# Sixteen first-product units and four block products as 64-row halves on both halves of the array

## The chip, the cores and the metric

The kernel runs on one core of one Trainium2 chip. That core has five engines with instruction queues of their own: PE (TensorE, the 128x128 matmul array, with a separate weight load that the profile lists as PEld), DVE (VectorE), ACT (ScalarE), POOL (GpSimd) and SP (SyncE, which here only starts DMAs). Matmuls write to PSUM, which has eight banks; DVE and ACT read results from there.

The metric is the device time of one execution in microseconds (us), as the median of several runs. A profile is one further execution under the hardware profiler. Its page and its trace give the span from the first to the last instruction.

## The reference

Attention over normalised queries and keys, and behind it a dense block with a hard-swish between its two products. In outline:

```python
# q, k, v: (batch 8, heads 12, seq 448, head_dim 64); tau = 0.1
q_n = q / (norm(q) + 1e-6)
k_n = k / (norm(k) + 1e-6)
scores = q_n @ k_n.T / tau
attn = softmax(scores)                 # with 1e-9 beside the sum
o = attn @ v
x = o as rows of tokens                # (3584, 768): 8 batches of 448 tokens
# w_in: (768, 2048), w_out: (2048, 768)
h = x @ w_in                           # "first product"
g = h * clip(h + 3, 0, 6) / 6
out = g @ w_out                        # "second product"
```

## The kernel before

**Units.** The work behind the attention is cut into units, and each unit is a run of matmuls into one PSUM bank, followed by what empties the bank.

- A *first-product unit* (`mm1_unit`, matmuls at L598) makes one of the 16 blocks of 128 columns of `h` for one batch: six matmuls (768 = 6 x 128 rows) of 128 rows by 448 tokens into one bank. ACT then computes `u = relu(h/6 + 0.5)` from the bank (`relu`, L614), and DVE computes `min(u, 1) * h` from `u` and the bank (`product`, L620) into `g`. Only after that is the bank free.
- The second product is done by a scheme with seven block products for a pair of token blocks, where eight would be usual. Sums and differences of blocks of `g` (`g_sum`, DVE, L772) and of `w_out` come first. A *block product* (`product_unit`, matmuls at L794) is eight matmuls of 128 rows by 384 columns. Its name has a digit 1 to 7 and the number of the pair: 2.9 is block product 2 of pair 9. Products 2, 5 and 6 accumulate in the bank that holds 4, 3 and 1 of the same pair. Product 1 is added to a buffer by DVE (L851), 6 and 7 are added by DVE into an output tile that is stored (L819), 2 to 5 are copied by ACT (L813, L842), and POOL combines buffers (L823 to L827).
- A *single unit* (`single_unit`, L874) is 16 matmuls for half the columns of one token block that has no partner.

**Banks.** Two of the eight banks hold the attention's values (PV). The other six (M0, M1, Y, Z, M2, M3 in this order) form a ring: each new unit that does not accumulate takes the next bank (`next_bank`, L160, through `bank_of`, L321). A matmul into a bank that is still being read waits for the reader.

**Order.** Each engine executes its queue in the order in which the program issues it; nothing is scheduled later. The order of the attention's start is a written list (`PLAN`), then a loop goes over pairs of heads and mixes units into the attention by `TURNS`. Behind the last attention stands the list `units[NP]` (L984 to L993), which is run by `whole_units` (L1034): it issues a unit's matmuls and then at once the instructions that empty its bank (`post`, one list each for ACT, DVE and POOL). Dependencies between engines become semaphore waits where the data require them.

The part of `units[NP]` that the change touches (L987 to L989) runs, in this order: first-product unit 0 of the last batch, block product 2.9, unit 1, 1.9, unit 2, 7.9, unit 3, 6.9, and then units 4 to 15 one behind the other. The two single units `s6.0` and `s6.1` follow, with DVE's sums for pair 10 between them, and then the block products of pairs 10 and 11, which read what the 16 first-product units made.

**Halves in the kernel before.** A matmul may use 64 of the array's 128 rows. The attention's scores (L445) do: the contraction is 64 long, and two matmuls of 64 rows, one on rows 0 to 63 and one on rows 64 to 127, stand beside one another in the queue, into two banks. Part of the values (L486) do the same.

Of the kernel before, what the change touches and what calls it, by code (L numbers as in the profile page):

```python
# [64 lines left out]
def kernel(  # L65
# [10 lines left out]
    nc = tc.nc  # L76
    B, H, S, D = q.shape
# [4 lines left out]
    NP = B * HP  # L82
    CC = d_model // 128
    FCN = d_ff // 128
# [17 lines left out]
    w_in_sb = const.tile([128, CC, d_ff], BF16, name="w_in_sb", tag="w_in_sb")  # L102
# [4 lines left out]
    KC = FCN // 2  # L107
# [60 lines left out]
    def needs(*what):  # L168
        for w in what:
            assert w in issued or any(x < 0 for x in w[1:] if isinstance(x, int)), w  # L170

    halves = {}
# [148 lines left out]
    def bank_of(name, reads):  # L321

        bank = {"Y": Y, "Z": Z}[name] if name else next_bank()
        key = id(bank)
        assert not unread.get(key), name
        unread[key] = reads
        return bank, key
# [228 lines left out]

    evac_n = [0]
    post = {"a": [], "v": [], "p": []}
    g_done = set()

    def tail(c, n):
# [8 lines left out]
    def g_of(b):  # L570
        if b == B - 1:
            needs(("NM", NP - 1), ("RE", NP - 1), ("VC", NP - 1))
            return g_last
        return gT[b % 2]
# [16 lines left out]
    def mm1_unit(b, fc, ends=None):  # L591
        needs(*(("CX", i) for i in range(b * HP, (b + 1) * HP)))
        assert len(weights) <= 8 - 2 * min(2, 4 * fc // FCN)
        x, g, c0 = xT[b % 2], g_of(b), b % 2 * SR
        ps, key = bank_of(None, 1)
        def products_of(ccs):
            for cc in ccs:
                nc.tensor.matmul(  # L598
                    ps[:, 0:S],
                    w_in_sb[:, cc, fc * 128 : (fc + 1) * 128],  # L600
                    x[:, cc, 0:S],
                    start=(cc == 0),
                    stop=(cc == CC - 1),
                )

        if ends is None:
            products_of(range(CC))
        else:
            products_of(range(CC - 1))
            ends.append(lambda: products_of([CC - 1]))  # L610

        def relu():
            u = sb.tile([128, S], BF16, name="u", tag="u", bufs=3)
            nc.scalar.activation(  # L614
                out=u[:, :], in_=ps[:, 0:S], func=AF.Relu, bias=0.5, scale=1.0 / 6.0
            )
            post["v"].append(lambda: product(u))

        def product(u):
            nc.vector.scalar_tensor_tensor(  # L620
                out=g[:, fc, c0 : c0 + S],
                in0=u[:, :],
                scalar=1.0,
                in1=ps[:, 0:S],
                op0=ALU.min,
                op1=ALU.mult,
            )
            unread[key] = 0
            g_done.add((b, fc))

        post["a"].append(relu)
# [78 lines left out]
    def sum_of(n, what):  # L710

        if what == "e":
            return late_sums[1]["e"]
        if n < LOOP or n == LAST:
            return gs[what + str(n % 2 if n not in (3, 5) else 0) if what == "7" else what]
        return late_sums[n % 2][what]
# [32 lines left out]
    def block(n, i, k):  # L749
        if PAIRS[n][i] == (2, 2):  # L750
            return kept[k]
        return half(*PAIRS[n][i], k)
# [22 lines left out]
    def product_unit(n, name, end=None, apart=False):  # L775

        need = {"3": ["y3"], "4": ["y4"], "1": "1", "6": "6", "7": "7"}.get(name, [])
        assert all((x, c) in summed for x in need for c in range(KC))
        if name not in "34":
            assert (n, name) in g_summed  # L780
        base = None if apart else {"2": "4", "5": "3", "6": "1"}.get(name)
        if base is None:
            banks[n, name] = bank_of(None, 1)
        ps, key = banks.pop((n, base)) if base else banks[n, name]
        c0, width = (MH // 2 * end, MH // 2) if end in (0, 1) else (0, MH)
        if name in "167":
            lhs, rhs = sum_of(n, name), w_sum[name]
        else:
            i, k = {"3": (0, 0), "4": (1, 1), "2": (1, 0), "5": (0, 1)}[name]
            m = LEFT if name in "42" else RIGHT  # L790
            lhs, rhs = block(n, i, k), w_out_sb[:, :, m].rearrange("p (c k) m -> p c k m", k=2)[:, :, k, :]
        m = ps[:, c0 : c0 + width]
        for c in range(KC):
            nc.tensor.matmul(  # L794
                m,
                lhs[:, c, :],
                rhs[:, c, c0 : c0 + width],
                start=(base is None and c == 0),
                stop=(c == KC - 1),
                skip_group_check=True,  # L800
            )
        issued_products.add((n, name))
        d, e = d_and_e(n)
        if base is None and name in "34":
            unread[key] = 1 + ((n, name) not in APART)

        def done(i, o, cols):
            unread[key] = 0
            result(*PAIRS[n][i], cols, o, end)

        def copied(i, cols):
            o = out_tile()
            nc.scalar.copy(out=o[:, :], in_=m)  # L813
            parts[n, name] = o
            done(i, o, cols)

        def added(i, cols, x):
            parts[n, name] = o = out_tile()
            nc.vector.tensor_tensor(out=o[:, 0:width], in0=m, in1=x[:, c0 : c0 + width], op=ALU.add)  # L819
            done(i, o, slice(cols.start + c0, cols.start + c0 + width))  # L820

        def both():
            nc.gpsimd.tensor_tensor(out=e, in0=d, in1=e, op=ALU.add)  # L823
            nc.gpsimd.tensor_tensor(out=d, in0=e, in1=parts[n, "5"][:, :], op=ALU.subtract)

        def rest():
            nc.gpsimd.tensor_tensor(out=e, in0=e, in1=parts[n, "2"][:, :], op=ALU.subtract)  # L827

        def added_later(i, cols, x):
            parts[n, name] = o = out_tile()  # L830
            nc.scalar.copy(out=o[:, :], in_=m)
            unread[key] = 0

            def add():
                nc.gpsimd.tensor_tensor(out=o[:, :], in0=o[:, :], in1=x, op=ALU.add)
                result(*PAIRS[n][i], cols, o)

            post["p"].append(add)

        def finish():  # L840
            if name in "34":
                nc.scalar.copy(out={"3": d, "4": e}[name], in_=m)  # L842
                unread[key] -= 1
            elif apart:
                added_later(*{"5": (0, RIGHT, d), "2": (1, LEFT, e)}[name])
            elif name == "5":
                copied(0, RIGHT)
            elif name == "2":
                copied(1, LEFT)
            elif name == "1":  # L850
                nc.vector.tensor_tensor(out=d, in0=m, in1=d, op=ALU.add)  # L851
            elif name == "6":
                added(1, RIGHT, e)
            else:
                added(0, LEFT, d)
            ready.add((n, name))
            first = {(n, x) for x in ("245" if (n, "4") in APART else "45")}
            if (n, name) in first and first <= ready:
                post["p"].append(both)
            if name in "245" and {(n, "4"), (n, "5"), (n, "2")} <= ready:  # L860
                post["p"].append(rest)

        post["a" if name in "2345" else "v"].append(finish)
# [26 lines left out]
    def sums(n, names):  # L890
        return [(g_sum, n, x) for x in names]
# [4 lines left out]
    def products(text):  # L896

        u = []
        for x in text.split():
            name, n = x.split(".")  # L900
            if name[0] == "s":
                u.append((single_unit, int(name[1]), int(n)))
            else:
                u.append((product_unit, int(n), name[0], None, name[1:] == "a"))
        return u
# [58 lines left out]
    units = {}  # L964
    rest_of = firsts(1, FCN - 1) + [u for b in range(2, B - 1) for u in firsts(b, *range(FCN))]
    for i, text in TURNS.items():
        units[i] = []
        for x in text.split():
# [5 lines left out]
            elif x[0] == "+":  # L974
                name, n = x[1:].split(".")
# [7 lines left out]
    f = firsts(b, *range(FCN))  # L983
    units[NP] = sums(8, "1") + carry[:1] + products("4.8") + carry[1:] + [(g_left, B - 2)] + products("2.8")  # L984
    units[NP] += products("3.9") + sums(9, "75") + products("1.8 4.9") + sums(9, "62") + products("6.8 5.9") + sums(9, "1")
    units[NP] += products("7.8") + sums(B - 2, "e")
    for n, x in enumerate("2176"):  # L987
        units[NP] += f[n : n + 1] + products(x + ".9")
    units[NP] += f[4:] + products(f"s{B - 2}.0") + sums(10, "75") + products(f"s{B - 2}.1") + sums(10, "62")  # L989
    units[NP] += products("3.10 4.10") + sums(10, "1") + products("5.10") + sums(11, "75") + products("2.10 3.11") + sums(11, "62")  # L990
    units[NP] += products("4.11 5.11") + sums(11, "1") + products("2.11 1.10 1.11")
    units[NP] += [(product_unit, n, x, 2) for n, x in ((10, "7"), (10, "6"), (11, "6"))]
# [38 lines left out]
    def finish_units(e):  # L1031
        post[e].pop(0)()
# [56 lines left out]
    for i in range(FIRST, NP):  # L1089
# [40 lines left out]
        n = 2  # L1130
# [64 lines left out]
```

## Time and profile before

| | before |
|---|---|
| time, median of 2 runs | 401.69 us (401.65 to 401.73) |
| span of the profiled execution | 399.5 us |
| the profiled execution's own time | not given beside its span; the median is 2.2 us above the span |
| PE busy | 391.4 us, 98% of the span, 3673 matmuls |
| DVE, ACT, POOL busy | 291.1, 274.3, 235.9 us |
| stretch that the change rewrites | 348.61 to 371.96 us from the span's start |

How to read the lines that follow. In the page, the first numbers of an engine are its busy time and share of the span. "PEclk" is the clock granted to TensorE in tenths, for 40 equal slices of the span. The line of percentages is the chain of work that ended last, by engine. A line of the waits reads: engine, line and tile of the waiting instruction, what it waited for, us in total, times, longest. A line of the timeline reads: start in us from the span's start, us, engine, line of the kernel, operation, out<-in, shape, count; in brackets the idle time of that engine just before, and what ended it. Instructions of one kind that follow one another are merged, and the us then reach from the first start to the last end. A matmul's us reach from its start to the end of its last result; the next matmul starts before that. A line of windows reads: from:to, length, busy us and count of PE, PEld, DVE, ACT and POOL, granted clock, share of the DMA engines, GB/s.

### The profile page before, as it was taken

To read this page: it belongs to the slowest core of one execution; us is meant where nothing else is said; L and a number is where in the kernel's file an instruction comes from. 1 tells how busy PE (TensorE), PEld (TensorE's weight loads), DVE (VectorE), ACT (ScalarE), POOL (GpSimd) and SP (SyncE) were. 2 spreads that over 40 slices of the span, in tenths; PEclk is the share of its full clock that TensorE was granted. 3 is DMA by queue.
4 is the path that set the end of the run, shared out by engine and by line. 5 is a ranking of instruction groups with operands and counts; after the bars stand their busy time and mean duration, and the time that the engine had idled before them with its cause. 6 is when DMAs were issued, how large, how long until landed. Compare 5 with 4: busy or idle time off the path is not lost.

```text
span 399.5 us, 9623 instructions
## 1 busy us (share of the span) xinstructions
PE 391.4 (98%) x3673; PEld 230.9 (58%) x3673; DVE 291.1 (73%) x514; ACT 274.3 (69%) x627; POOL 235.9 (59%) x234
## 2 busy tenths in 40 slices
PE   7999999999999999999999999999999999999996
PEld 5656466555555556555555555555565556555563
DVE  6898988889878597766878775976766565645663
ACT  6899998886887676887776776767658655224230
POOL 7897229652853989579859829688396500400070
PEclk9999999999999999999999999999999999999999
DMA  8999987797987678795888386694953424230133
GB/s 292 291 226 252 240 188 206 149 172 193 222 201 171 159 193 183 174 231 152 196 178 230 81 203 158 155 198 136 193 125 75 103 48 67 46 74 21 31 71 97
DMA packets 92365, 63.73 MB, mean 160 GB/s; under 512 B 56096, under 2 KB 91552, under 8 KB 92320
## 3 DMA queue, kind: packets, MB, share of 16 engines
q1 hardware_dynamic: 87408, 56.45, 58.6%
q0 software_dynamic: 4512, 6.29, 9.3%
q8 instruction: 28, 0.46, 0.5%
q10 hardware_dynamic: 400, 0.39, 0.3%
q14 instruction: 17, 0.14, 0.1%
HBM read 45.61 MB, written 11.01 MB: 142 GB/s over the span
## 4 chain that ended last, share of the span: by engine, by line
PE 90%; ACT 5%; DMA 1%; DVE 1%; POOL 1%; issue 0%; SPq 0%; ACTq 0%
PE M L598 24%; PE M L794 19%; PE PV L486 11%; PE Y L598 6%; PE Z L598 6%; PE M L445 5%; PE Z L794 5%; PE Y L794 4%; ACT at L463 4%; PE Z L445 1%; PE Y L445 1%; PE M L874 1%; PE PV L1016 1%; DMA big<-in_q_dram 1%; POOL nrm L297 1%; PE Z L659 1%
## 5 line engine op out<-in xcount | busy, mean ns | idle before, releaser
L598 PE MATMUL M<-xT,w_in_sb 128*128 128x448 bf16 x522 | 110.7, 353 | 0.1
L598 PEld LDWEIGHTS <-w_in_sb 128*128 128x128 bf16 x768 | 72.0, 98 | 62.2 <-issue 1.9
L463 ACT ACTIVATE at<-M 128x448 bf16<-128x448 f32 x192 | 96.4, 569 | 16.7 <-PE M L445 15.7
L297 POOL TENSOR_TENSOR nrm<-big,r 128x896 bf16<-128x896 f32 (+1 forms) x46 | 77.1, 1680 | 27.8 <-ACT r L260 10.7
L229 POOL TENSOR_TENSOR big<-big 128x896 f32<-128x896 f32 (+3 forms) x41 | 60.8, 1488 | 16.6 <-DVE n L241 11.0
L620 DVE SCALAR_TENSOR_TENSOR gT<-u,M 128x448 bf16<-128x448 bf16 x76 | 46.2, 616 | 32.0 <-ACT u L614 31.8
L614 ACT ACTIVATE u<-M 128x448 bf16<-128x448 f32 x87 | 48.5, 560 | 28.3 <-PE M L598 27.9
L486 PEld LDWEIGHTS <-at 128*128 128x128 bf16 (+1 forms) x1536 | 53.0, 97 | 22.8 <-issue 14.4
L486 PE MATMUL PV<-vx,at 128*128 128x65 bf16 (+1 forms) x1536 | 62.3, 193 | 0.3 <-DVE on L507 0.2
L241 DVE TENSOR_REDUCE n<-big 128x14 f32<-128x896 f32 (+1 forms) x50 | 51.7, 1041 | 5.7 <-POOL big L229 3.9
L794 PEld LDWEIGHTS <-gT 128*128 128x128 bf16 x336 | 32.5, 98 | 23.3 <-issue 0.4
L823 POOL TENSOR_TENSOR big<-big 128x384 f32<-128x384 f32 x13 | 13.4, 1034 | 53.7 <-ACT big L842 53.5
L794 PE MATMUL M<-w_out_sb,gT 128*128 128x384 bf16 x224 | 40.2, 326 | 0.0
L794 PEld LDWEIGHTS <-gs 128*128 128x128 bf16 x280 | 27.0, 98 | 18.7 <-issue 0.5
L402 POOL COPY km<-tT 64x128 bf16<-64x128 bf16 x34 | 14.0, 413 | 34.7 <-PE M L445 9.7
L507 DVE TENSOR_TENSOR on<-PV,rc 128x512 bf16<-128x512 f32 x48 | 33.2, 691 | 1.7
L794 PE MATMUL M<-w_sum,gs 128*128 128x384 bf16 (+1 forms) x192 | 34.2, 323 | 0.0
L463 ACT ACTIVATE at<-Y 128x448 bf16<-128x448 f32 x52 | 29.6, 569 | 6.0 <-PE Z L445 5.9
L445 PE MATMUL M<-tT,kz 64*128 64x448 bf16 x169 | 31.1, 351 | 0.3 <-DVE gT L620 0.2
L463 ACT ACTIVATE at<-Z 128x448 bf16<-128x448 f32 x50 | 28.8, 576 | 0.4 <-PE M L445 0.4
L598 PE MATMUL Y<-xT,w_in_sb 128*128 128x448 bf16 x126 | 27.4, 353 | 0.0
L316 POOL CAST vx<-big 128x512 bf16<-128x512 f32 x36 | 24.1, 672 | 4.9 <-DMA big<-in_v_dram 4.9
(137 smaller groups left out, 563.1 us busy)
## 6 DMA issues: line engine op xcount, KB each, us to landing
big<-in_k_dram SPq DMA_DIRECT2D x24, 448.0 KB, 4.5
big<-in_q_dram SPq DMA_DIRECT2D x24, 448.0 KB, 4.2
out_dram<-o SPq DMA_DIRECT2D x107, 96.0 KB, 2.2
big<-in_v_dram SPq DMA_DIRECT2D x48, 128.0 KB, 4.2
big<-in_v_dram SPq DMA_DIRECT2D x48, 96.0 KB, 4.1
w_out_sb<-in_moe_w_out_dram POOLq DMA_DIRECT2D x4, 768.0 KB, 9.4
w_in_sb<-in_moe_w_in_dram POOLq DMA_DIRECT2D x4, 384.0 KB, 10.7
w_in_sb<-in_moe_w_in_dram POOLq DMA_DIRECT2D x2, 768.0 KB, 21.5
```

Source lines behind the costliest of these rows:

```text
L229: engines[e].tensor_tensor(out=o, in0=i, in1=i, op=ALU.mult)
L241: nc.vector.tensor_reduce(out=n2s[d % 2][:, j % 2, c], in_=sq[:, :, :, :].rearrange("p g c d -> p (g c) d")[:, c, :], axis=AX.X, op=ALU.add,)
L297: engines[e].tensor_tensor(out=nrm[:, :, g, :].rearrange("p c g d -> p g c d"), in0=raw_of[j][:, g, :, :], in1=rs[d % 2][3][:, j % 2, :] . ...
L316: (engines[e].copy if e == "a" else engines[e].tensor_copy)(out=o, in_=f)
L445: nc.tensor.matmul(o, ks, qt[rows], start=True, stop=True)
L463: nc.scalar.activation(out=o, in_=x, func=AF.Exp, scale=inv_tau)
L486: nc.tensor.matmul(pv_out(j, h), at[rows, n, q_cols(i // HP, j)], vt[rows, 3 + h if name == "M" else 5 * h + int(name[1]), :], start=(name ...
L507: nc.vector.tensor_tensor(out=on[:, :, :, :].rearrange("p j h d -> p h j d"), in0=pv4[:, :, :, 0:D], in1=rc[:, :, :].to_broadcast([128, 2, ...
L598: nc.tensor.matmul(ps[:, 0:S], w_in_sb[:, cc, fc * 128 : (fc + 1) * 128], x[:, cc, 0:S], start=(cc == 0), stop=(cc == CC - 1),)
L614: nc.scalar.activation(out=u[:, :], in_=ps[:, 0:S], func=AF.Relu, bias=0.5, scale=1.0 / 6.0)
L620: nc.vector.scalar_tensor_tensor(out=g[:, fc, c0 : c0 + S], in0=u[:, :], scalar=1.0, in1=ps[:, 0:S], op0=ALU.min, op1=ALU.mult,)
L794: nc.tensor.matmul(m, lhs[:, c, :], rhs[:, c, c0 : c0 + width], start=(base is None and c == 0), stop=(c == KC - 1), skip_group_check=True,)
```

## The change

`accumulate` takes the place of the matmul loop in `product_unit` and of the loop in `mm1_unit` when that is run by the new function `in_lanes`. `in_lanes` takes two lists of units. It first calls each unit to learn its matmuls, and holds back both the matmuls and the instructions that empty the bank. It then issues each matmul as two of 64 rows: half 0 of the array (rows 0 to 63) runs the first list and then the second, half 1 (rows 64 to 127) the second list and then the first. The two halves' matmuls are put into one queue by a count of columns plus six for each matmul. Both halves of a unit accumulate in the unit's one bank, at different times; where a unit passes from one half to the other, PE is made to wait for the last matmul of the half before, by a nop whose wait ends up as an instruction of PE's queue. When a unit's last half matmul is issued, the instructions that empty its bank follow.

Five groups are run in this way: units 0 and 1 with block products 2.9 and 1.9; units 2 and 3 with 7.9 and 6.9; units 4 and 5 with 6 and 7; 8 and 9 with 10 and 11; 12 and 13 with 14 and 15. By the program's order, PE's queue has 128 more matmuls and weight loads; the queues of POOL and SP are as before, and in those of ACT and DVE only the instructions of this stretch stand in another order. The order in which units take banks from the ring: units 0, 1 and 1.9 take M2, M3, M0; units 2, 3 and 7.9 take M1, Y, Z; then units 4 to 15 M2, M3, M0, M1, Y, Z and again. 2.9 accumulates in 4.9's bank Y and 6.9 in 1.9's bank M0.

```diff
+    lane_ops = []
+
+    def accumulate(out, ops, fresh=True):
+        if lane_ops:
+            lane_ops[-1].append((out, ops, fresh))
+            return
+        for n, (lhs, rhs) in enumerate(ops):
+            nc.tensor.matmul(
+                out, lhs, rhs, start=(fresh and n == 0), stop=(n == len(ops) - 1), skip_group_check=True
+            )
+
+    HALVES = (slice(0, 64), slice(64, 128))
+
+    def in_lanes(first, second):
+        jobs = []
+        for f, *args in first + second:
+            before = {e: len(post[e]) for e in post}
+            lane_ops.append([])
+            f(*args)
+            (out, ops, fresh), = lane_ops.pop()
+            ends = [(e, post[e].pop()) for e in post if len(post[e]) > before[e]]
+            jobs.append([out, ops, fresh, 2 * len(ops), ends])
+        order = jobs, jobs[len(first) :] + jobs[: len(first)]
+        halves = []
+        for h, mine in enumerate(order):
+            at = 0
+            for job in mine:
+                out, ops, *_ = job
+                for n in range(len(ops)):
+                    halves.append((at, h, n, job))
+                    at += out.shape[-1] + 6
+        for at, h, n, job in sorted(halves, key=lambda x: x[:2]):
+            out, ops, fresh, left, ends = job[:5]
+            lhs, rhs = ops[n]
+            if job[5:] and job[5] != h:
+                info = mybir.DependencyInfo(mybir.DependencyClass.Sync, mybir.DependencyReason.DATA)
+                wait = nc.tensor.nop(nofuse=True)
+                tc.add_manual_dep(wait.ins, job[6].ins.name, info, reason="one half of the array at a time in a bank")
+            ins = nc.tensor.matmul(
+                out,
+                lhs[HALVES[h]],
+                rhs[HALVES[h]],
+                start=(fresh and left == 2 * len(ops)),
+                stop=(left == 1),
+                skip_group_check=True,
+            )
+            job[3] -= 1
+            job[5:] = h, ins
+            if not job[3]:
+                for e, f in ends:
+                    post[e].append(f)
+                for e in "avp":
+                    while post[e]:
+                        finish_units(e)
...
-        if ends is None:
+        if lane_ops:
+            accumulate(
+                ps[:, 0:S], [(w_in_sb[:, cc, fc * 128 : (fc + 1) * 128], x[:, cc, 0:S]) for cc in range(CC)]
+            )
+        elif ends is None:
             products_of(range(CC))
...
-        for c in range(KC):
-            nc.tensor.matmul(
-                m,
-                lhs[:, c, :],
-                rhs[:, c, c0 : c0 + width],
-                start=(base is None and c == 0),
-                stop=(c == KC - 1),
-                skip_group_check=True,
-            )
+        accumulate(m, [(lhs[:, c, :], rhs[:, c, c0 : c0 + width]) for c in range(KC)], base is None)
...
-    for n, x in enumerate("2176"):
-        units[NP] += f[n : n + 1] + products(x + ".9")
-    units[NP] += f[4:] + products(f"s{B - 2}.0") + sums(10, "75") + products(f"s{B - 2}.1") + sums(10, "62")
+    for n, x in enumerate(("2.9 1.9", "7.9 6.9")):
+        units[NP].append((in_lanes, f[2 * n : 2 * n + 2], products(x)))
+    for n in range(4, FCN, 4):
+        units[NP].append((in_lanes, f[n : n + 2], f[n + 2 : n + 4]))
+    units[NP] += products(f"s{B - 2}.0") + sums(10, "75") + products(f"s{B - 2}.1") + sums(10, "62")
```

## The prediction

> **What bounds the kernel now.** I read the page from the top: busy time, slices, chain, then the waits of PE, then the stretch that the diff rewrites.
>
> ```profile
> span 399.5 us, 9623 instructions
> PE 391.4 (98%) x3673; PEld 230.9 (58%) x3673; DVE 291.1 (73%) x514; ACT 274.3 (69%) x627; POOL 235.9 (59%) x234
> PEclk9999999999999999999999999999999999999999
> PE 90%; ACT 5%; DMA 1%; DVE 1%; POOL 1%; issue 0%; SPq 0%; ACTq 0%
> ...
> PE PV L1016 <- DVE vx L1067: 2.5, 1, 2.5
> PE M L445 <- DVE gT L620: 0.2, 1, 0.2
> ...
> 348.61:371.96 23.35, 23.35 (x129) 12.52 (x128) 11.87 (x20) 8.63 (x16) 1.51 (x2) 1.00 0.21 47
> 371.96:377.16 5.20, 5.20 (x33) 3.13 (x32) 2.74 (x5) 0.54 (x1) 0.00 (x0) 1.00 0.11 24
> ```
>
> PE is busy 98% of the span and is 90% of the chain; of PE's five waits the longest is 2.5 us at the very start, the last of the list 0.2, and none lies in the tail. The two windows show the changed stretch (16 first-product units, 4 block products: 23.35 us, PE busy throughout, DVE at half, ACT at a third, clock 1.00) and the two single units behind it. A busy PE need not stream at its peak, so the next rows look at start to start.
>
> ```profile
> 348.61 1.30 PE L598 MATMUL M<-xT,w_in_sb 128*128 128x448 bf16 x6
> 349.74 1.46 PE L794 MATMUL Y<-w_out_sb,gT 128*128 128x384 bf16 x8
> 351.04 1.30 PE L598 MATMUL M<-xT,w_in_sb 128*128 128x448 bf16 x6
> ...
> 369.69 1.30 PE L598 MATMUL Y<-xT,w_in_sb 128*128 128x448 bf16 x6
> 370.83 1.30 PE L598 MATMUL Z<-xT,w_in_sb 128*128 128x448 bf16 x6
> 371.96 1.46 PE L874 MATMUL M<-w_out_sb,big 128*128 128x384 bf16 x8
> ```
>
> A first-product unit F takes 1.13 us for six matmuls (189 ns each), a block product 1.30 us for eight (162.5 ns). 64 columns more cost 26.5 ns, so a column costs 0.414 ns, and 189 less 448 of them leaves about 3 ns per matmul that is not streaming. That is all that better overlap could win: 3 ns on 128 matmuls, 0.4 us.
>
> **The change part by part.** *Matmuls.* 128 whole-height matmuls (16x6 + 4x8) become 256 of 64 rows with the same columns. Whether they cost nothing or double depends on both halves streaming at once. The attention scores (L445) have such pairs.
>
> ```profile
> 114.42 0.31 PE L486 MATMUL PV<-vx,at 128*128 128x65 bf16 x5
> 114.67 0.36 PE L445 MATMUL Z<-tT,kz 64*128 64x448 bf16 x1
> ...
> 197.53 0.35 PE L445 MATMUL Y<-tT,kz 64*128 64x448 bf16 x1
> 197.53 0.35 PE L445 MATMUL M<-tT,kz 64*128 64x448 bf16 x1
> 197.72 0.35 PE L445 MATMUL Z<-tT,kz 64*128 64x448 bf16 x1
> 197.79 0.35 PE L445 MATMUL M<-tT,kz 64*128 64x448 bf16 x1
> 198.06 0.42 PE L486 MATMUL PV<-vx,at 128*128 128x65 bf16 x8
> ```
>
> Two halves start at the same hundredth (197.53) and the next follows 0.19 later: a pair costs what one whole matmul of that width costs. At 197.72 and 197.79 they start 0.07 apart and still overlap, so they need not go in step. Pairs therefore cost as before, 23.35 us. Bounds: 0.4 us less if the fixed 3 ns hide; 10 ns more per pair (0.20 for 0.19) on 128 pairs, 1.3 us more. Halves of unlike width (448 beside 384, in the first two groups) are in no row; forced into step they would take 12x189 + 4x162.5 + 12x189 = 5.19 us a group for 4.87, 0.6 us in both.
>
> *Change of shape.* From whole rows to halves: five value matmuls take 0.31 with a last one of some 0.19, so the last starts at 114.54, and the next at 114.67, 0.13 later where 0.03 is usual: 0.10 us. Back: 197.79 to 198.06, 0.27 where 0.19 is usual: 0.08, I take 0.10. The stretch is entered once and left once: **0.2 us**.
>
> *Waits within the array.* Before a unit passes to the other half, PE waits for the last matmul of the first half in that bank. By the order that started over a unit (1.1 us) before, with 0.35 us to its end: met, nothing. If not, each of the 20 passages costs a fraction of 0.35.
>
> *When banks come free.* Before, units end one by one, 1.13 us apart, and a bank is reused six units later. Now four units share a group and end late, two by two: half 0 runs first pair, second pair; half 1 the reverse. The next group needs four banks of six at once. So I follow the evacuation with these rows.
>
> ```profile
> 350.00 0.54 ACT L614 ACTIVATE u<-M 128x448 bf16<-128x448 f32 x1 [2.02 <-PE M L598]
> 350.58 0.62 DVE L620 SCALAR_TENSOR_TENSOR big<-u,M 128x448 bf16<-128x448 bf16 x1 [0.61 <-ACT u L614]
> ...
> 343.68 0.56 DVE L851 TENSOR_TENSOR big<-M,big 128x384 f32<-128x384 f32 x1
> 344.15 0.68 DVE L772 TENSOR_TENSOR big<-gT 128x1024 bf16<-128x1024 bf16 x1
> ...
> 321.87 0.56 DVE L819 TENSOR_TENSOR o<-M,big 128x384 f32<-128x384 f32 x1 [0.16 <-PE M L794]
> 322.48 0.98 ACT L463 ACTIVATE at<-M 128x448 bf16<-128x448 f32 x2 [1.42 <-PE M L445]
> 322.49 0.36 PE L445 MATMUL M<-tT,kz 64*128 64x448 bf16 x2
> ```
>
> F's matmuls stop being issued at 349.74; its relu starts at 350.00: 0.26 later. The product (L620) starts 0.58 after the relu and takes 0.62. Behind one another, a DVE instruction starts 0.09 before the recorded end of the one ahead (343.68 + 0.56 against 344.15), two 0.56 us activations 0.42 apart (0.98 for both). DVE's end frees PE some 0.05 later (321.87 + 0.56 = 322.43, and 322.49). Let 0 be the first matmul of the stretch; with the change of shape, group 1 starts at 0.10.
>
> Group 1 (F0 F1 | 2.9 1.9) takes 2x1.135 + 2x1.30 = 4.87, to 4.97; F1 and 1.9 end there together. F1's relu starts at 5.23, its product runs 5.81 to 6.43, and 1.9's addition (L851), behind it on DVE, 6.34 to 6.90. Group 2 (F2 F3 | 7.9 6.9) has 6.9 accumulating in 1.9's bank. Half 1 comes to it after 7.9, at 6.27, and waits until 6.95: **0.68**. PE issues in order, so half 0 stands behind it.
>
> Group 2 ends at 4.97 + 4.87 + 0.68 = 10.52 with F3 and 6.9. F3's relu at 10.78, product 11.36 to 11.98, 6.9's addition 11.89 to 12.45. The ring gives that bank to F6, half 1's first unit in group 3 (F4 F5 | F6 F7): wanted at 10.52, free at 12.50: **1.98**.
>
> Group 3 runs 4x1.135 = 4.54 more, to 17.04. Its third units end one earlier: F4 (half 1) at 15.90, F6 on half 0 0.19 before that. Relus at 15.97 and 16.39, products 16.55 to 17.17 and 17.08 to 17.70. F10, half 1's first of group 4 (F8 F9 | F10 F11), has F4's bank: wanted at 17.04, free at 17.75: **0.71**. F11 has F5's, the fourth product (18.22 to 18.84): free at 18.89 and wanted at 18.88, nothing. Group 5 meets group 4 the same way: **0.71**. It ends at 17.04 + 2x(0.71 + 4.54) = 27.54, the stretch at 27.64.
>
> Behind it, the last product is done 1.8 us into the single units' 5.20, well ahead of the products that read it; loads, stores and the order on SP and POOL stay. The waiting PE has behind it only its own matmuls. **Sum: 27.64 - 23.35 = 4.3 us** (waits 4.1, shape 0.2). The page gives a span of 399.5 and no time of its own for that execution; the median, 401.69, is 2.2 longer, launch and end around the span. So a span of 403.8 and **406.0 us**.
>
> **The rivals.** *The banks come free in time* (the waits are mis-scheduled by me): then 0.2 us, 401.9. For it: PE waits for nothing in the tail now. Against: the two-by-two ends and DVE's order follow from the code.
>
> *Slower by over 2%: the halves take turns when they differ.* If a 448-wide matmul of one half and a 384-wide one of the other do not overlap, groups 1 and 2 take 9.74 longer; 6.9 then finds its bank free (2.60 of cover for 1.98), the other waits stay (1.98 + 1.42), with 0.2 for shape: 13.3, 415.0. If no accumulating pair overlaps, all double: 23.35 + 1.98 + 0.2, 427.2 (F10 and F14 then have 2.27 of cover for 1.85). It decides where a second half starts only after the first has streamed its 0.19. Against it: 197.72 and 197.79. For it: those rows do not accumulate and are of equal width.
>
> *The clock.* PE stands 2 us, then 0.7 twice.
>
> ```profile
> 394.73 0.82 PE L794 MATMUL Y<-w_sum,gs 128*128 128x192 bf16 x8
> 395.50:398.70 3.20, 0.05 (x1) 0.00 (x0) 0.36 (x1) 0.00 (x0) 0.00 (x0) 1.00 0.49 125
> 398.70:399.50 0.80, 0.00 (x0) 0.00 (x0) 0.00 (x0) 0.00 (x0) 0.00 (x0) 0.54 0.00 0
> ```
>
> The last matmul ends at 395.55 and the granted clock falls only after 398.70, 3.2 us later; a gap of 2.0 stays below. Should it fall, 3.2 us of work at about half rate costs 1.6: 407.6. The Trainium skill ("TensorE: Matmul & The Clock Gate", Part 1) states the same rule against idle PE: after an idle window of about 3.4 us the clock is halved until PE has been busy as long. By that rule 2.0 us alone does nothing; the trace agrees so far with its 3.2.
>
> **How the numbers follow.** Forecast 0.79 (406.0), banks in time 0.07 (401.9), unlike halves in turns 0.05 (415.0), all in turns 0.04 (427.2), clock 0.04 (407.6), anything else 0.01. Range: four waits uncertain by 0.2 each (0.8), below also the 0.4, above the 1.3 and 0.6: 404.8 to 408.7; it takes in the clock and leaves out 0.17. About 2% (8.0 us) is what a measurement of this kernel tells from no change: faster 0.01, same 0.90, slower 0.09.
>
> **What would show it.** Pairs of 64-row matmuls starting together, 0.19 apart; four gaps on PE: 0.7 released by the addition of L851, 2.0 by that of L819, twice 0.7 by products of L620; the single units 4.3 us later than 371.96. A region of over 33 us says that halves take turns; no gap and an equal region that the banks are free. I am wrong if a gap falls elsewhere, or if the waits inside the array show.

## The result and the profile after

| | before | after |
|---|---|---|
| time, median of 2 runs | 401.69 us (401.65 to 401.73) | 406.62 us (406.52 to 406.73) |
| ratio after to before | | 1.0123, 95% interval 1.0094 to 1.0152 |
| span of the profiled execution | 399.5 us | 404.6 us |
| stretch: end of 7.8 to first single unit | 23.36 us | 27.49 us |

The change makes the kernel 4.9 us slower (1.2%, interval 3.8 to 6.1 us), which is within the 2% that was called no change. In the new file the product unit's matmuls are at L567, the halves at L599, the single units at L926, the relu at L674, the product at L680, and the two kinds of addition at L903 (into the running sum, L851 before) and L871 (into the output tile, L819 before).

First the head of the page of the kernel after, and from its list of waits the rows of PE at the halves (L599):

```profile
span 404.6 us, 9887 instructions
PE 392.9 (97%) x3801; PEld 234.1 (58%) x3801; DVE 291.8 (72%) x514; ACT 273.6 (68%) x627; POOL 235.8 (58%) x234
PEclk9999999999999999999999999999999999999999
...
PE M L599 <- DVE o L871: 1.6, 1, 1.6
PE M L599 <- DVE big L680: 0.5, 1, 0.5
PE Y L599 <- DVE big L680: 0.5, 1, 0.5
PE M L599 <- DVE big L903: 0.4, 1, 0.4
```

PE has 128 more matmuls and almost the same busy time, so halves do not cost double. Four new waits have come in the stretch, one behind L903, one behind L871 and two behind L680, and no others. (The list has one more row that is not in the list of before, 0.2 us at L1070 at 56.4 us, in the attention; the same kernel run again does not have it.) The four add up to 3.0 us here, but a wait is counted from the modelled end of the last matmul; what is lost is read from start to start. So the timeline of PE, kernel after, at the way in, at the four waits and at the way out:

```profile
347.83 1.46 PE L567 MATMUL Z<-w_sum,gs 128*128 128x384 bf16 x8
349.23 0.36 PE L599 MATMUL M<-xT,w_in_sb 64*128 64x448 bf16 x1
349.23 0.49 PE L599 MATMUL Y<-w_out_sb,gT 64*128 64x384 bf16 x2
349.42 0.35 PE L599 MATMUL M<-xT,w_in_sb 64*128 64x448 bf16 x1
...
355.24 0.35 PE L599 MATMUL Y<-xT,w_in_sb 64*128 64x448 bf16 x1
355.25 0.32 PE L599 MATMUL Z<-w_sum,big 64*128 64x384 bf16 x1
356.02 0.32 PE L599 MATMUL M<-w_sum,big 64*128 64x384 bf16 x1 [0.43 <-DVE big L903]
...
359.42 0.32 PE L599 MATMUL M<-w_sum,big 64*128 64x384 bf16 x1
359.59 0.35 PE L599 MATMUL M<-xT,w_in_sb 64*128 64x448 bf16 x1
361.50 4.70 PE L599 MATMUL M<-xT,w_in_sb 64*128 64x448 bf16 x47 [1.57 <-DVE o L871]
365.87 0.35 PE L599 MATMUL Y<-xT,w_in_sb 64*128 64x448 bf16 x1
366.76 0.35 PE L599 MATMUL M<-xT,w_in_sb 64*128 64x448 bf16 x1 [0.54 <-DVE big L680]
...
371.14 0.35 PE L599 MATMUL M<-xT,w_in_sb 64*128 64x448 bf16 x1
371.98 0.35 PE L599 MATMUL Y<-xT,w_in_sb 64*128 64x448 bf16 x1 [0.49 <-DVE big L680]
...
376.33 0.35 PE L599 MATMUL M<-xT,w_in_sb 64*128 64x448 bf16 x1
376.62 1.47 PE L926 MATMUL M<-w_out_sb,big 128*128 128x384 bf16 x8
```

The last whole product, 7.8, has eight matmuls at 162.5 ns, so it stops being issued at 347.83 + 1.30 = 349.13; the single units begin at 376.62. The stretch is 27.49 us. (That of before is 23.36 by the unrounded starts, 23.35 by the printed ones.) Its extra 4.13 us over before are made up as follows; the losses too are taken from unrounded starts and can differ from the printed ones by 0.01. Where a start would have followed anyway one turn later (0.16 to 0.19), that turn is taken off:

| place | from, to | lost |
|---|---|---|
| way in, change of shape | 349.13, 349.23 | 0.10 |
| 6.9 behind 1.9's addition, L903 | 355.25, 356.02 | 0.61 |
| F6 behind 6.9's addition, L871 | 359.59, 361.50 | 1.92 |
| F10 behind a product, L680 | 365.87, 366.76 | 0.72 |
| F14 behind a product, L680 | 371.14, 371.98 | 0.67 |
| way out, change of shape | 376.33, 376.62, less 0.19 | 0.09 |
| sum | | 4.11 |

At F6 nothing is taken off: 359.59 is half 0's first matmul of group 3, and half 1 wanted its first one beside it. Between the waits the halves run at full pace: 47 matmuls from 361.50 take 4.70 us as printed, which is 4.35 from the first start to the last, 23 pairs at 0.189.

Why a bank is late is seen on DVE, same kernel, ahead of the first two waits and of the last:

```profile
354.88 0.62 DVE L680 SCALAR_TENSOR_TENSOR big<-u,M 128x448 bf16<-128x448 bf16 x1 [0.26 <-ACT u L674]
355.42 0.55 DVE L903 TENSOR_TENSOR big<-M,big 128x384 f32<-128x384 f32 x1
...
360.36 0.62 DVE L680 SCALAR_TENSOR_TENSOR big<-u,Y 128x448 bf16<-128x448 bf16 x1 [0.51 <-ACT u L674]
360.90 0.55 DVE L871 TENSOR_TENSOR o<-M,big 128x384 f32<-128x384 f32 x1
...
370.78 0.62 DVE L680 SCALAR_TENSOR_TENSOR big<-u,M 128x448 bf16<-128x448 bf16 x1 [2.92 <-ACT u L674]
371.32 0.61 DVE L680 SCALAR_TENSOR_TENSOR big<-u,Y 128x448 bf16<-128x448 bf16 x1
```

At the first two waits a first product and a block product end together, and the addition that frees the bank stands behind the product on DVE: it starts 0.54 after the product does, the two end at 355.97 and 361.45, and PE starts 0.05 later both times. That product in turn waited for its relu, while DVE had nothing else to do (0.26 and 0.51 idle). The last matmul of 6.9 starts at 359.42 and ends by the trace at 359.74, so the second addition ran 1.16 us behind its data. At the last wait two first products end close together. DVE had been idle for 2.92 us, and F8's product, which frees the bank for F14, is the second of the two: it ends at 371.93, and PE starts 0.05 later. F10's bank is freed by the second product of its group in the same way.

The clock, in the windows of the same kernel (columns as before: the clock is the third number from the end):

```profile
360.00:366.00 6.00, 4.50 (x48) 2.71 (x48) 1.53 (x3) 1.31 (x3) 0.00 (x0) 1.00 0.31 70
366.00:371.00 5.00, 4.46 (x50) 2.52 (x47) 2.08 (x5) 1.77 (x4) 0.00 (x0) 1.00 0.00 0
```

It stays at 1.00 across the wait of 1.9 us and behind it.

### The profile page after: what moved, and what is told of

The parts are those of the page before. It is cut to its first block, busy times and chain, and to the rows that moved or that the text cites. A ratio compares the mean times of both kernels' runs of the same rounds, so it can differ in the third digit from the quotient of the medians.

```text
span 404.6 us, 9887 instructions
## 1 busy us (share of the span) xinstructions
PE 392.9 (97%) x3801; PEld 234.1 (58%) x3801; DVE 291.8 (72%) x514; ACT 273.6 (68%) x627; POOL 235.8 (58%) x234
## 5 line engine op out<-in xcount | busy, mean ns | idle before, releaser
L654 PE MATMUL M<-xT,w_in_sb 128*128 128x448 bf16 x456 | 97.4, 353 | 0.1
L654 PEld LDWEIGHTS <-w_in_sb 128*128 128x128 bf16 x672 | 62.7, 98 | 53.7 <-issue 1.9
L680 DVE SCALAR_TENSOR_TENSOR gT<-u,M 128x448 bf16<-128x448 bf16 x76 | 46.1, 616 | 32.3 <-ACT u L674 32.2
L674 ACT ACTIVATE u<-M 128x448 bf16<-128x448 f32 x87 | 48.3, 560 | 29.8 <-PE M L654 17.2
L875 POOL TENSOR_TENSOR big<-big 128x384 f32<-128x384 f32 x13 | 13.5, 1036 | 56.6 <-ACT big L894 56.4
L567 PEld LDWEIGHTS <-gT 128*128 128x128 bf16 x328 | 31.8, 98 | 22.7 <-issue 0.4
L567 PE MATMUL M<-w_out_sb,gT 128*128 128x384 bf16 x224 | 40.2, 326 | 0.0
L567 PEld LDWEIGHTS <-gs 128*128 128x128 bf16 x280 | 27.0, 98 | 18.6 <-issue 0.4
L567 PE MATMUL M<-w_sum,gs 128*128 128x384 bf16 (+1 forms) x192 | 34.2, 323 | 0.0
L654 PE MATMUL Y<-xT,w_in_sb 128*128 128x448 bf16 x114 | 24.8, 353 | 0.0
```

What stands on the lines that cost most here:

```text
L567: nc.tensor.matmul(out, lhs, rhs, start=(fresh and n == 0), stop=(n == len(ops) - 1), skip_group_check=True)
L654: nc.tensor.matmul(ps[:, 0:S], w_in_sb[:, cc, fc * 128 : (fc + 1) * 128], x[:, cc, 0:S], start=(cc == 0), stop=(cc == CC - 1),)
L674: nc.scalar.activation(out=u[:, :], in_=ps[:, 0:S], func=AF.Relu, bias=0.5, scale=1.0 / 6.0)
L680: nc.vector.scalar_tensor_tensor(out=g[:, fc, c0 : c0 + S], in0=u[:, :], scalar=1.0, in1=ps[:, 0:S], op0=ALU.min, op1=ALU.mult,)
```

## The experiments

The four with several timed runs (the change again, and the first three edits) ran beside the same 21 runs of before, median 402.13 us. The next four ran once each (402.04, 406.74, 404.12 and 407.14 us, in the order below) beside one run of before at 402.75, so their stretches are read and not their times. "Stretch" is always from 1.30 us behind the start of 7.8's row to the first single unit. The theory is that all the loss is the four waits for banks, plus the change of shape. The rival causes are the halves themselves, their unlike widths, and the waits within the array.

**The change again.** The kernel as it is.

> The changed kernel once more, with more rounds, to size what lies outside the stretch. Its first profile: the stretch with its two changes of shape took 27.49 us (from the end of the last whole-row product at 349.13 to the first single unit at 376.62) for 23.36 before, 4.1 more, while the span was 5.1 longer: 0.5 of that lay at the very start (clock of the first matmuls) and 0.5 behind the last matmuls (an output tile waiting for its store). If those are chance, the time over several rounds is 401.7 + 4.1 = 405.8 and the profile shows another start and tail; if they belong to the change, it stays at 406.6 and the same start and tail come back.

Measured: 407.34 us (4 runs, 406.24 to 408.96), ratio 1.0121 (1.0091 to 1.0150). The stretch is 27.48 us, with the same gaps to 0.01 us, so what the change does inside the stretch comes back. Neither of the two expected outcomes came for the rest. The time is 5.2 us above before (3.7 to 6.0), 1.1 more than the stretch explains. The start and the tail did not come back the same: in the profiled run, which took 408.96, the row of 7.8 starts 2.1 us later than in the profile of before, and from the first single unit to the end of the span it takes 29.0 us, for 28.0 in the first profile of the change and 27.5 before.

**The block products in the other order.** 1.9 and 6.9 now come first in half 1, so that neither ends together with a first product, and the bank of each is free a unit earlier.

```diff
-    for n, x in enumerate(("2.9 1.9", "7.9 6.9")):
+    for n, x in enumerate(("1.9 2.9", "6.9 7.9")):
```

> The two block products of each of the first two groups change places (1.9 before 2.9, 6.9 before 7.9), nothing else; 1.9 then ends one unit earlier, and so does 6.9. Banks theory: the gap before 6.9 (0.6 us in the changed kernel's profile) and the one before unit 6 (1.9) go, the two gaps of 0.7 stay: 2.5 us less than the changed kernel, about 404.1 (with 405.8 as its base 403.3). If the halves themselves or the passages from half to half cost the time: no change, 405.8 to 406.6.

Measured: 403.88 us (6 runs), ratio 1.0045 (1.0029 to 1.0060), stretch 25.15. The two waits behind the additions are gone; the timeline of PE in this kernel runs into the third group without a gap, and in the stretch its list of waits has only the two behind products left. The rows at F10 follow behind those of the third group:

```profile
359.34 1.88 PE L599 MATMUL M<-xT,w_in_sb 64*128 64x448 bf16 x18
...
363.88 0.35 PE L599 MATMUL Y<-xT,w_in_sb 64*128 64x448 bf16 x1
364.77 0.35 PE L599 MATMUL M<-xT,w_in_sb 64*128 64x448 bf16 x1 [0.54 <-DVE big L680]
...
374.61 1.47 PE L926 MATMUL M<-w_out_sb,big 128*128 128x384 bf16 x8
```

```profile
PE M L599 <- DVE big L680: 0.5, 1, 0.5
PE Y L599 <- DVE big L680: 0.5, 1, 0.5
```

So 2.34 us of the 4.13 came from the order of two names in each of two strings. The stretch is some 0.17 longer than expected (2.5 less than in the kernel after). In the kernel after, half 0 leads through group 3, so that half 1 would have come to F10 one turn (0.17) behind 365.87 anyway. Without the wait at F6 the halves are level, no turn is taken off, and half 1 loses the whole 0.89 there (363.88 to 364.77).

**Eight banks instead of six.** Behind the last attention the two banks of the values' sums (PV) are closed and opened again as two more tiles at the end of the ring.

```diff
-    PV = psum.tile([128, 2, 512], FP32, name="PV", tag="PV")
+    values_pool = ExitStack()
+    psum_v = values_pool.enter_context(tc.tile_pool(name="psum_v", bufs=1, space=bass.MemoryType.PSUM, side="right"))
+    PV = psum_v.tile([128, 2, 512], FP32, name="PV", tag="PV")
...
+    do("UU", [u[0] for u in stream].index(in_lanes), "avp")
+    values_pool.close()
+    psum_w = ctx.enter_context(tc.tile_pool(name="psum_w", bufs=1, space=bass.MemoryType.PSUM, side="right"))
+    at = ring_n[0] % len(ring)
+    ring[:] = ring[at:] + ring[:at] + [psum_w.tile([128, 512], FP32, name=f"W{n}", tag=f"W{n}") for n in range(2)]
+    ring_n[0] = 0
```

> The order of the change, but behind the last attention the ring of banks gets the two banks of the attention's values as seventh and eighth member. Banks theory: only the gap before 6.9 stays (it accumulates in 1.9's bank, which no further bank helps): 401.7 + 0.2 (two changes of shape) + 0.6 = 402.5, and the profile shows one gap on PE of 0.6 us. Halves or passages cost the time: no change, 405.8 to 406.6.

Measured: 403.93 us (10 runs), ratio 1.0042 (1.0016 to 1.0068), stretch 24.17 us. The one expected wait is left in the stretch, that of 6.9 for 1.9's bank, which the ring does not give out; the list of waits of this kernel has it as its only row at a half:

```profile
PE M L601 <- DVE big L905: 0.4, 1, 0.4
```

So F6, F10 and F14 waited for banks and for nothing else.

**Both edits together.**

> Both at once, the changed order of the block products and eight banks. Banks theory: no gap is left in the stretch, 401.7 + 0.2 = 401.9, the stretch 23.6 us. If halves of unlike width or the waits from half to half cost something of their own, it shows here as what is left above 401.9: unlike widths in step 0.6 us (402.5), ten waits in PE's queue at 0.05 to 0.35 each 0.5 to 3.5 (402.4 to 405.4).

Measured: 403.73 us (10 runs), ratio 1.0039 (1.0018 to 1.0060), stretch 23.60 for 23.6. By the time alone this kernel would lie in the range that was given to waits in PE's queue (402.4 to 405.4); it is the stretch that tells the two apart. The complete list of PE's waits in this kernel has none at a half (L601 here) any more:

```profile
PE PV L1072 <- DVE vx L1123: 2.5, 1, 2.5
PE SC L447 <- ACT at L465: 0.4, 1, 0.4
PE PV L488 <- DVE on L509: 0.2, 1, 0.2
PE M L447 <- DVE gT L682: 0.2, 1, 0.2
```

This is the price of the halves by themselves: 23.60 for 23.36 us, 0.20 for the change of shape and 0.04 for 128 pairs of matmuls, unlike widths and 20 passages from half to half included. It is also the most that these groups can give: no matmul became cheaper, and even without any wait the stretch is longer than before.

**One kind of group alone.** First only the two groups with block products; then only the three of first products, with the rest as before.

```diff
-    for n in range(4, FCN, 4):
-        units[NP].append((in_lanes, f[n : n + 2], f[n + 2 : n + 4]))
+    units[NP] += f[4:]
```

> One part alone: the two groups with block products run as halves, units 4 to 15 whole. Banks theory: the gap before 6.9 (0.6) stays, unit 6 finds its bank free since units 4 and 5 (2.3 us) stand between (needed: 1.9). Stretch 23.4 + 0.2 + 0.6 = 24.2 us, one gap. If halves of unlike width cost something of their own: more than that by up to 0.6 (in step).

```diff
-    for n, x in enumerate(("2.9 1.9", "7.9 6.9")):
-        units[NP].append((in_lanes, f[2 * n : 2 * n + 2], products(x)))
+    for n, x in enumerate("2176"):
+        units[NP] += f[n : n + 1] + products(x + ".9")
```

> The other part alone: units 4 to 15 run as halves in groups of four, units 0 to 3 and the block products whole. Banks theory: unit 6, first on half 1, needs the bank of 6.9, which ended whole just before and has its addition alone in DVE's queue: 0.26 + 0.56 + 0.05 = 0.9; then the two gaps of 0.7. Stretch 23.4 + 0.2 + 0.9 + 1.4 = 25.9 us, three gaps; with e5 the parts then make 0.8 + 2.5 = 3.3 of the 4.1, the rest being the longer wait where both meet.

Measured: stretches of 24.19 and 25.72 us for 24.2 and 25.9, that is 0.83 and 2.36 over before. The waits in the second kernel's timeline of PE, and the addition on DVE that ends the first of them:

```profile
361.25 0.36 PE L599 MATMUL M<-xT,w_in_sb 64*128 64x448 bf16 x1
362.02 4.70 PE L599 MATMUL M<-xT,w_in_sb 64*128 64x448 bf16 x47 [0.41 <-DVE o L871]
...
367.28 0.35 PE L599 MATMUL M<-xT,w_in_sb 64*128 64x448 bf16 x1 [0.54 <-DVE big L680]
```

```profile
361.41 0.56 DVE L871 TENSOR_TENSOR o<-M,big 128x384 f32<-128x384 f32 x1 [0.16 <-PE M L567]
```

The two parts do not add up to the whole (3.19 for 4.13, with the change of shape counted twice). What is missing is in the wait at F6. Here, in the second kernel, 6.9 is a whole unit, its addition starts as soon as it ends, and F6 loses 0.77; in the kernel after, the addition stands behind a product that ended together with it, and F6 loses 1.92.

**Passages without a unit between them.** Groups of two first products: each half passes straight from one bank to the one that the other half has just left.

```diff
-    for n, x in enumerate(("2.9 1.9", "7.9 6.9")):
-        units[NP].append((in_lanes, f[2 * n : 2 * n + 2], products(x)))
-    for n in range(4, FCN, 4):
-        units[NP].append((in_lanes, f[n : n + 2], f[n + 2 : n + 4]))
+    for n, x in enumerate("2176"):
+        units[NP] += f[n : n + 1] + products(x + ".9")
+    for n in range(4, FCN, 2):
+        units[NP].append((in_lanes, f[n : n + 1], f[n + 1 : n + 2]))
```

> Units 0 to 3 and their block products run whole as before; units 4 to 15 run as halves in groups of two instead of four, so that a unit passes to the other half right behind the last matmul of the half before, and a bank is used again only three groups later. Banks theory: no gap of 0.7 or 1.9; the wait from half to half, which cost nothing in groups of four, is now in the open: 0.35 (a matmul to its end) + 0.05 - 0.19 (its own turn) = 0.2 for each of six groups. Stretch 23.4 + 0.2 (shape) + 6 x 0.2 = 24.8 us. Rival, that a wait in PE's own queue empties it and costs more than the matmul's end (0.5 each): 26.6. Rival, that it was these waits that cost the 4.1: longer than 27.5.

Measured: stretch 25.53 us, 0.7 more than expected. The timeline of PE and the list of waits, this kernel:

```profile
358.76 1.31 PE L599 MATMUL M<-xT,w_in_sb 64*128 64x448 bf16 x12
360.22 2.45 PE L599 MATMUL M<-xT,w_in_sb 64*128 64x448 bf16 x24 [0.15 <-PE M L599]
362.82 1.31 PE L599 MATMUL M<-xT,w_in_sb 64*128 64x448 bf16 x12 [0.15 <-PE M L599]
```

```profile
PE M L599 <- PE M L599: 0.5, 3, 0.2
```

Six pairs start from 358.76 to 359.72 (1.31 less the 0.35 of the last one), and the next starts at 360.22: 0.50 from start to start where 0.19 is usual. The halves wait for each other's last matmul to its end (0.35) and 0.15 more. The list names three such waits; the starts show the same 0.50 at all six passages. Six passages at 0.31 are 1.86, and with 0.2 for shape they give 25.4 of the 25.53. I had put the step behind the end at 0.05, as DVE's frees PE; PE's own takes three times that. So a wait within the array is dear where it is met. In the change it is not met, because a whole unit lies between.

**One half after the other.** Units 4 to 7 run all six matmuls of half 0, then wait, then all six of half 1; nothing of the same unit lies beside them.

```diff
+    def in_turns(unit):
+        f, *args = unit
...
+        for h in range(2):
+            if h:
+                ...
+                wait = nc.tensor.nop(nofuse=True)
+                tc.add_manual_dep(wait.ins, ins.ins.name, info, reason="one half of the array at a time in a bank")
+            for n, (lhs, rhs) in enumerate(ops):
+                ins = nc.tensor.matmul(
...
+    for n, x in enumerate("2176"):
+        units[NP] += f[n : n + 1] + products(x + ".9")
+    for n in range(4, 8):
+        units[NP].append((in_turns, f[n]))
+    units[NP] += f[8:]
```

> The price of a half that has nothing beside it: units 4 to 7 run first on half 0 of the array and then on half 1, one unit after the other; all others run whole. If a 64-row matmul takes as long as one of 128 rows (both 0.19): 4 x 1.13 = 4.5 more, 0.2 for shape, 0.2 for each of four passages, less 0.19 at three places where the next unit's first half can start beside the last matmul of the other half: 4.5 + 0.2 + 0.8 - 0.6 = 4.9, stretch 28.3 us. If a half alone took half the time: 23.4 + 0.2 + 0.8 = 24.4.

Measured: stretch 27.13 us, 1.2 below the theory and 2.7 above the rival. The timeline of PE, this kernel:

```profile
360.25 1.30 PE L626 MATMUL M<-xT,w_in_sb 64*128 64x448 bf16 x6
361.70 1.69 PE L626 MATMUL M<-xT,w_in_sb 64*128 64x448 bf16 x12
363.54 1.69 PE L626 MATMUL M<-xT,w_in_sb 64*128 64x448 bf16 x12
```

The first row settles the price: six halves alone take 1.30, as six whole matmuls do, so a half that has nothing beside it saves nothing. The second row shows where my sum was wrong. Twelve matmuls, half 1 of one unit and half 0 of the next, start within 1.69 - 0.35 = 1.34 us. In the order of the queue the next unit's would begin only beside the last of half 1 or behind it, and the twelve would take at least 5 x 0.19 + 5 x 0.19 = 1.9. They overlap by 0.56 more, three matmuls. The single starts in the trace fall into two series, each 0.19 from start to start: one from 361.70, the other from 362.09, and the last of the second is 0.40 behind the last of the first. So PE began the next unit's half 0 while three matmuls that stand ahead of it in the queue had not begun. Three such overlaps (-1.7) and four passages at 0.50 for 0.40 (+0.4) give 27.0.

**The kernel before, three more times,** to see what differs outside the stretch.

> The kernel before, profiled again, to see how much of a difference between two profiled runs lies outside the stretch. Theory (the time ahead of the stretch and behind it varies from run to run, whatever the kernel): the stretch is 23.36 us to 0.03, the row of 7.8 starts anywhere from 347.2 to 350.2, and the three profiles of this kernel differ from each other in it by over 0.3 us. Rival (the change delays the start): all three start that row within 0.15 us of 347.31.

> As the first of the three: stretch 23.36 us; by the theory the start of 7.8's row differs by over 0.3 us from at least one of the other two, by the rival it is within 0.15 us of 347.31.

> As the first of the three: stretch 23.36 us; by the theory the start of 7.8's row differs by over 0.3 us from at least one of the other two, by the rival it is within 0.15 us of 347.31.

Measured: 401.37, 401.96 and 401.92 us, one run each. 7.8's row starts at 347.18, 347.59 and 347.59; the stretch is 23.36 in all three. The rows of the first and of the second, timeline of PE:

```profile
347.18 1.46 PE L794 MATMUL Z<-w_sum,gs 128*128 128x384 bf16 x8
...
371.84 1.46 PE L874 MATMUL M<-w_out_sb,big 128*128 128x384 bf16 x8
```

```profile
347.59 1.46 PE L794 MATMUL Z<-w_sum,gs 128*128 128x384 bf16 x8
...
372.25 1.46 PE L874 MATMUL M<-w_out_sb,big 128*128 128x384 bf16 x8
```

So the time ahead of the stretch varies by 0.41 us in the kernel before too, as the theory said. One wait at the start of the program (L342, for POOL) varies along with it: it lists 0.2 in the first, 0.6 in the second and 0.8 in the third. In the changed kernel run again it lists 1.1, and there the row of 7.8 starts at 349.40 for 347.83. That does not put the rival away altogether: over the nine profiles of changed kernels the row starts at 347.23 to 350.12, while the four profiles of before lie between 347.18 and 347.59. That a changed kernel also tends to start the stretch later is neither shown nor excluded.

## Why the prediction was right

Forecast 406.0 us by four waits for banks and a change of shape; measured 406.62. The mechanism came out as forecast, but that the time is so close is in part luck: the stretch grew by 4.13 for 4.29, and 0.8 us of the 4.93 lie outside it, where the forecast had nothing. Each step, and what the runs say of it:

- **Pairs cost as whole matmuls:** right. With all waits taken out, 128 pairs cost 0.04 us (23.60 - 23.36 - 0.20). Neither bound came: the fixed 3 ns were not hidden, and no pair was 10 ns dearer. A half alone takes the whole 0.19 (the run with one half after the other), so two halves must overlap fully just to cost what one whole matmul costs.
- **Unlike widths:** right that they need not go in step. In the first group each half keeps its own pace: in the rows at 349.23 the 448-wide half has its second start 0.19 later (349.42), while two of the 384-wide, 0.32 long each, are merged into 0.49, that is 0.16 to 0.17 apart. So the rival at 415.0 is out, and that at 427.2 with it.
- **Change of shape, 0.2:** right, 0.10 in and 0.09 out. The Trainium skill ("TensorEngine Tiling (Array Packing)", Key Properties) says that a change of tiling mode drains TensorE. The trace prices it at about 0.1 us each way, so it is nothing to avoid where it is done once; the drain itself it does not show, since at both places the next matmul starts before the recorded (modelled) end of the last one (349.23 against 347.83 + 1.46 = 349.29, and 376.62 against 376.68).
- **Waits within the array, nothing:** right for this change. Had they been met, my price was too low: "a fraction of 0.35" for each was, where groups of two met them, 0.31 more than the usual distance from start to start, but through 0.15 behind the end that I had not counted.
- **The four bank waits, 4.1:** right in place, in releaser and in order, 3.9 in size. 0.68 was 0.61: 6.9 found its bank 6.89 us behind the start of the stretch (356.02 - 349.13) where the sum over relu, product and addition had 6.95. 1.98 was 1.92, by the same 0.06; 0.71 was 0.72, and 0.71 was 0.67. The ones said to be nothing (F11, F15) are nothing. Taking their causes away one by one, by order and by banks, took away each wait that was meant and no other; with the other order F10's grew by 0.17, as told there.
- **Everything behind unchanged:** right up to the last matmuls. The span grew by 5.1 and not 4.3. Of the 1.0 beyond the measured 4.13, 0.52 lies ahead of the stretch (347.83 for 347.31) and 0.48 behind it. The first is a little over the spread of 0.41 that the kernel before shows against itself. The second goes with one row on DVE at the very end, in the kernel after and in its second profile:

```profile
400.96 0.36 DVE L871 TENSOR_TENSOR o<-Y,big 128x192 f32<-128x192 f32 x1 [0.96 <-DMA out_dram<-o]
```

```profile
401.81 0.36 DVE L871 TENSOR_TENSOR o<-Y,big 128x192 f32<-128x192 f32 x1 [0.25 <-PE Y L567]
```

In one profile the last addition waited for a store; in the other, and in all profiles of before, for PE. Yet the second profile's tail is the longest of all, 1.5 us over before: there the last four stores land 3.4 to 4.0 us after their issue, for 1.9 to 2.2 in the profile of before. A longer tail shows up in three of the nine profiles of changed kernels, these two and that of eight banks (0.5 us); the other six take 27.5 us from the first single unit to the end, as all four of before do. So it varies from run to run and does not belong to the halves as such, but why it is in both profiles of the change and in none of before is open.

- **The clock:** right, 1.00 throughout the stretch.

One thing stays open. With the stretch only 0.24 us longer, the kernel with both edits was 1.6 us slower than before (0.7 to 2.4), and the one with eight banks 1.7 for 0.81. The runs of the first spread over 2.7 us and of the second over 3.7, as those of before do over 2.7, and I have not found where in the program the rest lies. The kernel with the other order alone has no such rest (1.8 for 1.79). What the two share and that one lacks is the values' pool, opened apart, closed and opened again, and the ring of eight banks; whether either matters was not tried. The change as it was also has a rest, 0.8 in the first pair of runs and 1.1 when run again, whose intervals (3.8 to 6.1 and 3.7 to 6.0) take in the 4.13.

No version has a shorter stretch than the kernel before: what could be won was 3 ns a matmul, and the halves did not win it.

## What to carry to other kernels

Halves of the array side by side give nothing where the whole height was in use already: the pair costs what the whole cost, and what changes is when results end. If units that used to end one by one end two by two, the engines that empty their banks get their work in bunches, and with a ring sized for the even flow PE waits though no engine is near its limit; then either give the bunch more banks or put first the unit whose bank is wanted next. Follow each bank from its last matmul over relu, product and addition, in the queue order of each engine, before regrouping.

## What the runs showed of the hardware that was not expected

PE waiting for its own matmul in the other half pays 0.50 us from start to start, 0.35 to the end of that matmul and 0.15 behind it; behind DVE it starts 0.05 after the end.

Matmuls of different halves do not start in the order of the queue: twelve starts in 1.34 us, where the order would need 1.9, mean that three were overtaken. So the rule stated ahead of the prediction, that an engine executes its queue in the order of issue, did not hold between the halves of PE in that run; why the next unit's half began after two matmuls and not at once is not shown. The Trainium skill ("TensorE: Matmul & The Clock Gate", Part 3) says that matmuls start and end strictly in order; these rows differ, and the measurement decides. A wait on the last matmul in the queue is therefore no proof that those of the other half ahead of it have ended.
